# Row moments by VectorE transposes, and another order of the weight loads and stores, in a fused attention and MLP kernel

## The chip, the cores and the metric

The kernel runs on one core of a Trainium2 chip. The metric is the device time of one execution in microseconds (us), as a median of several runs. The engines of the core run side by side, each with an instruction stream of its own, and wait for each other by semaphores: TensorE (PE in the profile, with its weight loads as PEld), VectorE (DVE), ScalarE (ACT), GpSimd (POOL), and SyncE (SP), whose stream here holds nothing but the issue of DMA transfers.

## The reference

One batch of 2048 tokens of width 576 goes through two branches, which a gate mixes. All arrays are float32.

```python
x = A_x
g = _sigmoid((x * gate_w).sum(-1, keepdims=True))
a = _A_ref(x, A_wqkv, A_wo)            # linear attention, 32 heads of 18
b = _B_ref(x, B_w1, B_b1, B_w2, B_b2)  # layer norm, 576 -> 4608, gelu, 4608 -> 576
return g * a + (1 - g) * b
...
def _B_ref(x, w1, b1, w2, b2):
    y = _layernorm(x, axis=-1)
    h = _gelu(jnp.einsum("bsd,df->bsf", y, w1) + b1)
    return jnp.einsum("bsf,fd->bsd", h, w2) + b2
```

## The kernel before, in words

The tokens lie in 16 tiles of 128, which the kernel takes in eight pairs. Every large product is made by float32r matmuls on a value split in two: ACT copies a block to float32r (the high part), DVE subtracts that from the source (the low part), and three products of the parts are summed in PSUM. Both MLP products are also made by a seven-product scheme on 2x2 blocks, which trades matmuls for sums of blocks: A11, A12, A22 and the sums S1 to S4 of w1; B11, B12, B21, B22 and the sums T1 to T4 on the other side.

**The attention part** (the first 305 us) walks over the tiles. For a tile, PE projects keys and queries, ACT and DVE make the feature map, PE adds up the products of keys and x. In the same walk the mean and the scale of the layer norm are found. For pair q they stand in `mr[:, q]`, a tile of 128 partitions by 8 pairs by 2 kinds by 2 tiles: one number for a token, and the token is the partition. `share_moments` (line 383) stores them to a DRAM tensor `moments[q]` of 2 rows of 256 numbers, and `load_rows` (line 399) loads these rows back to all partitions, so that `normal_pair` can normalise x in its transposed form. Each pair's normalised and split blocks go to DRAM (`yd`) by `store_pair`; the first two blocks of w1 are also split here and stored (`w1d`, by `store_early`). All these transfers are issued by SP, in the order of the program.

**The MLP part** is 18 windows of 14 steps (line 1145), run after the attention part. A step holds seven matmuls of 512 columns of the first product (`product`) and twelve of 288 columns of the second (`unit`), which runs one window behind. Two blocks k of w1 belong to a window, one to its steps 0 to 6 and one to its steps 7 to 13. The first nine windows work on the first half of the tokens and the last nine on the second half. In the first half a block of w1 is loaded raw, summed, split, used, and stored in its split form to `w1d[k]`, from where the second half loads it back; so the second half has no sums and no splits of w1.

What runs beside the matmuls is written as jobs on the steps (lines 1049 to 1142), and on each engine the jobs stand in program order. For w1 in the first half, with x the first step of block k in its window:

- `sum_w1` of block k + 1 (DVE, four sums, 128x384) at x to x + 3, into a raw buffer `w1_raw` (`w_raw` in the profile). S1, S2 and S4 = A12 − S2 need what is called the early part here, the raw blocks that `load_w1(…, True)` loads; S3 = A11 − S3 needs the late part, one raw block that `load_w1(…, False)` loads into the place of S3.
- at x + 4 `split_w1(k + 1, True)` into `wa` (ACT, then DVE), and eight DMAs for the early part of block k + 2. At x + 5 the store of `wa` to `w1d`.
- at x + 6 the split of the other blocks into `wb`, and then four DMAs for the late part of block k + 2; at x + 7 the store of `wb`.

For w2 there is one buffer `w2r` of seven places. `load_w2(p + 1)` (line 919) loads the four blocks of the next window at step 5, into the places of operands that the window has used up. POOL makes the four sums T3, T1, T2, T4 (`sum_w2`, 128x576), and behind them in its stream the sums of h (`sum_h`, on the tile `u`). `prepare_hi`, `prepare_h_lo` and `prepare_w2_lo` split an operand pair of the second product two steps ahead of its use (ACT and DVE, tiles `h` and `w_ops`), at every second step.

Of the kernel before, what the change touches and what calls it, by code (L numbers as in the profile page):

```python
# [9 lines left out]
F32 = mybir.dt.float32  # L10
# [7 lines left out]
P = 128  # L18
# [53 lines left out]
A11, A12, S2, S1, S3, A22, S4 = range(7)  # L72
A21 = S3
FIRST_W, LAST_W = (A11, S1), (S3, S4)
B11, B21, T1, B22, T2, T3, T4 = range(7)
# [7 lines left out]
HALF_PAIRS = NCHUNK // 2  # L83
# [17 lines left out]
def half_cols(half):  # L101
    return slice(half * HALF, (half + 1) * HALF)
# [14 lines left out]
def tile_gated_mix(ctx: ExitStack, tc: tile.TileContext, x, xm, xe, wm, we, wvm, wve, wo, um, ue, w2, b1, b2, gw, out):  # L117
    nc = tc.nc
    pe, act, dve, pool = (InOrder(tc, e) for e in (nc.tensor, nc.scalar, nc.vector, nc.gpsimd))
    sp = InOrder(tc, nc.sync)  # L120

    keep = ctx.enter_context(tc.tile_pool(name="keep", bufs=1))
# [48 lines left out]
    acc += [acc_right[:, i * D:(i + 1) * D] for i in range(TPS)]  # L171
    b1s = keep.tile([P, NFT], F32, name="b1s")
    mr = keep.tile([P, NP, 2, 2], F32, name="mr")
    sumsq = keep.tile([P, NT], F32, name="sumsq")
    gsum = keep.tile([P, NT], F32, name="gsum")
    g = keep.tile([P, NT], F32, name="g")
# [4 lines left out]
    moments = [dram.tile([2, 2 * P], F32, name=f"moments{q}") for q in range(NP)]  # L181
# [10 lines left out]
    for part in (KEY, QUERY):  # L192
        for half in range(2):
            n = HALF + 2 * (part == KEY and half)
# [186 lines left out]
        dve.tensor_mul(r, r, vr)  # L381

    def share_moments(q):
        sp.dma_start(moments[q].rearrange("a (t n) -> n a t", n=P), mr[:, q])

    B12 = T1
# [206 lines left out]
    def prepare_scale(q, n):  # L595
        at(n, scale_in, q)
        at(n + 1, scale_out, q)
        at(n + 2, share_moments, q)
# [32 lines left out]
    for n, f in ((50, scale_in), (56, scale_out), (56, share_moments)):  # L631
        at(n, f, NP - 1)
# [277 lines left out]
    w2r = own_tile("w2r", [P, 7, 2, HALF], F32)  # L910
    w2_ops = own_tile("w2_ops", [P, 2, 2, 2, HALF], F32R)
    free_ups, ups_at, w2_at = list(range(7)), {}, {}
# [3 lines left out]
    H_SUMS = {S3: (H11, H21, OP.subtract), S2: (H22, H21, OP.subtract), S1: (H22, H11, OP.add), S4: (H12, H22, OP.subtract)}  # L916
    W2_SUMS = {T3: (B22, B12), T1: (B12, B11), T2: (B22, T1), T4: (B21, T2)}

    def load_w2(p):
        old = w2_at.get(p - 1)  # L920
        new = w2_at[p] = dict(zip((B11, B21, T1, B22, T3, T2, T4),
                                  [old[m] for m in (B11, B21, T4, T3, T2, T1, B22)] if old else range(7)))
        first = 2 * p % NCHUNK * CF * P
        rows_ = w2[first:first + 2 * CF * P].rearrange("(j f p) d -> f p j d", j=2, f=CF)
        for f, blocks_ in enumerate(((B11, B12), (B21, B22))):
            for half, m in enumerate(blocks_):
                sp.dma_start(w2r[:, new[m]], rows_[f][:, :, half_cols(half)])

    def sum_w2(p, m, by=pool):
        of = lambda n: w2r[:, w2_at[p][n]]  # L930
# [120 lines left out]
    def do(w, x, f, *args):  # L1051
        jobs.setdefault((w + x // 14, x % 14), ([], []))[1].append(lambda: f(*args))

    def do_first(w, x, f, *args):
        jobs.setdefault((w + x // 14, x % 14), ([], []))[0].append(lambda: f(*args))
# [11 lines left out]
    for p in range(WINDOWS - 1):  # L1067
        w = p + 1
        if p == 0:
            for x, m in ((11, T3), (12, T1), (13, T2), (14, T4)):  # L1070
                do(0, x, sum_w2, 0, m, dve)
        for m in range(7):
            x = 2 * m - 2 - 2 * (p == m == 0)
            do_first(w, x, prepare_hi, p, m)
            do(w, x, prepare_h_lo, p, m)
            do(w, x, prepare_w2_lo, p, m)
        for x, m in ((0, S3), (3, S2), (6, S1), (7, S4)):
            do(w, x, sum_h, p, m)
        for x, m in ((4, S3), (8, S2), (9, S1), (11, S4)):
            do(w, x, give_back, p, m)  # L1080
        do(w, 5, load_w2, p + 1)
        if p + 1 < WINDOWS - 1:
            for x, m in ((9, T3), (10, T1), (11, T2), (12, T4)):
                do(w, x, sum_w2, p + 1, m)

    for k in range(HALF_TIME):
        w, x = k // 2, 7 * (k % 2)
        if k >= EARLY:
            do(w, x - 1, split_w1, k, False)
            if k + 1 < HALF_TIME:  # L1090
                do(w, x - 1, load_w1, k + 1, False)
            do(w, x, store_w1, k, False)
        if EARLY <= k + 1 < HALF_TIME:
            for n, x1 in enumerate((0, 1, 2, 3)):
                do(w, x + x1, sum_w1, k + 1, n, dve)
            do(w, x + 4, split_w1, k + 1, True)
            if k + 2 < HALF_TIME:
                do(w, x + 4, load_w1, k + 2, True)
            do(w, x + 5, store_w1, k + 1, True)

    p = HALF_PAIRS - 1
    for x, n, t in ((5, 2, 1), (10, 6, 1), (11, 7, 6), (12, 6, 5), (12, 4, 7), (13, 7, 5), (14, 3, 6)):
# [9 lines left out]
    h_stage = h_ops.rearrange("p c k a n -> p (c k a n)")  # L1112
    h_stages = [stage_of(h_stage[:, n * 10 * P:(n + 1) * 10 * P]) for n in range(3)]
    do(0, 0, load_w2, 0)
    u_stage = ups[:, 4:7].rearrange("p a j n -> p (a j n)").bitcast(F32R)
    u_stages = [stage_of(u_stage[:, n * 10 * P:(n + 1) * 10 * P]) for n in range(2)]
# [6 lines left out]
    p, w = WINDOWS - 1, WINDOWS - 1  # L1123
# [21 lines left out]
    for w in range(WINDOWS):  # L1145
        for x in range(14):
            k, i = 2 * w + x // 7, x % 7
# [3 lines left out]
            n, opens = UP_ORDER[i], (1, 2, 5) if w else (1, 2, 5, 4)  # L1151
# [14 lines left out]
    p = WINDOWS - 1  # L1166
# [66 lines left out]
```

## Time and profile before

| | |
|---|---|
| median of 3 runs | 1159.26 us (1158.85 to 1162.0) |
| the profiled execution | 1160.28 us, its span 1158.6 us |
| busy share of the span | PE 95%, PEld 86%, DVE 75%, ACT 49%, POOL 35% |
| granted TensorE clock, mean | 0.994 |
| HBM traffic | 135.95 MB read, 69.09 MB written |
| sizes of single DMAs | `w2r` 288 KB, store of `wa` 1280 KB, of `wb` 960 KB, raw w1 128 KB and 64 KB |

The span runs from the first to the last instruction; the time of an execution holds 1.7 us more. In the rows of a timeline stand the start in us, the busy time in us, the engine, line and operation, the tiles as out<-in, and in brackets the idle time ahead of it with what ended it. Rows of equal instructions are merged and end in their count. All work is recorded by one helper, so nearly every row has line 113, and a row is told by its tiles. A row of stages gives the stretch, its length, the busy time of PE, PEld, DVE, ACT and POOL, then PE's granted clock, the DMA engines' busy share, and GB/s.

### The profile page before, as it was taken

To read this page: it belongs to the slowest core of one execution; us is meant where nothing else is said; L and a number is where in the kernel's file an instruction comes from. 1 tells how busy PE (TensorE), PEld (TensorE's weight loads), DVE (VectorE), ACT (ScalarE), POOL (GpSimd) and SP (SyncE) were. 2 spreads that over 40 slices of the span, in tenths; PEclk is the share of its full clock that TensorE was granted. 3 is DMA by queue.
4 is the path that set the end of the run, shared out by engine and by line. 5 is a ranking of instruction groups with operands and counts; after the bars stand their busy time and mean duration, and the time that the engine had idled before them with its cause. 6 is when DMAs were issued, how large, how long until landed. Compare 5 with 4: busy or idle time off the path is not lost.

```text
span 1158.6 us, 18002 instructions
## 1 busy us (share of the span) xinstructions
PE 1104.6 (95%) x6651; PEld 997.1 (86%) x6651; DVE 868.8 (75%) x1201; ACT 567.9 (49%) x917; POOL 401.0 (35%) x276
## 2 busy tenths in 40 slices
PE   8988999899899999999998999999999999999998
PEld 8978898799777888888787888988999999999998
DVE  4676888798486979888798888688666666666587
ACT  6655675244464545445454554445444444444450
POOL 1101112783223333344233434425324424334310
PEclk9999999999999999999999999999999999999999
DMA  6489988886854364543546458856444344344342
GB/s 179 130 213 260 197 193 183 190 315 229 279 207 162 131 212 148 194 161 121 179 140 222 159 178 317 322 154 235 129 117 145 110 136 143 103 144 143 105 155 82
DMA packets 131133, 206.22 MB, mean 178 GB/s; under 512 B 13935, under 2 KB 86895, under 8 KB 127078
## 3 DMA queue, kind: packets, MB, share of 16 engines
q1 hardware_dynamic: 130482, 204.49, 56.9%
q8 instruction: 52, 0.85, 0.3%
q10 hardware_dynamic: 564, 0.59, 0.2%
q14 instruction: 35, 0.29, 0.1%
HBM read 135.95 MB, written 69.09 MB: 177 GB/s over the span
## 4 chain that ended last, share of the span: by engine, by line
PE 57%; DVE 18%; DMA 12%; issue 5%; SPq 4%; ACT 3%; POOL 0%; ACTq 0%; DVEq 0%; POOLq 0%
PE ps L113 57%; SPq L113 4%; DMA w_raw<-in_ue 4%; DVE wa L113 3%; DVE h L113 3%; DVE accs L113 3%; DVE w_ops L113 3%; DMA yd<-ys 1%; DMA w_raw<-in_um 1%; DVE den L113 1%; DMA w2r<-in_w 1%; ACT wa L113 1%; DMA xn<-in_x 1%; DMA wv<-in_wve 1%; DMA late_acc<-acc_right 1%
## 5 line engine op out<-in xcount | busy, mean ns | idle before, releaser
L113 PEld LDWEIGHTS ps<-w_ops,h 128*128 128x128 f32 x2856 | 429.0, 188 | 71.1 <-DVE w_ops L113 28.0
L113 PE MATMUL ps<-w_ops,h 128*128 128x288 f32 x2856 | 462.2, 297 | 21.2 <-DVE w_ops L113 19.2
L113 POOL TENSOR_TENSOR u<-u 128x512 f32<-128x512 f32 x136 | 212.8, 1592 | 273.0 <-DVE h L113 152.1
L113 PE MATMUL ps<-y,wa 128*128 128x512 f32 x1008 | 280.9, 395 | 5.7 <-DVE wa L113 2.8
L113 DVE TENSOR_TENSOR accs<-ps,accs 128x576 f32<-128x576 f32 x210 | 158.5, 755 | 98.7 <-PE ps L113 91.9
L113 ACT ACTIVATE u<-u,b1s 128x512 f32<-128x512 f32 x110 | 79.7, 725 | 269.3 <-DVE u L113 269.3
L113 PE MATMUL ps<-y,wb 128*128 128x512 f32 x756 | 203.3, 394 | 0.2
L113 PEld LDWEIGHTS ps<-y,wa 128*128 128x128 f32 x1008 | 173.7, 188 | 30.1 <-DVE wa L113 6.7
L113 POOL TENSOR_TENSOR w2r<-w2r 128x576 f32<-128x576 f32 x64 | 96.5, 1508 | 228.1 <-DMA w2r<-in_w 105.9
L113 PE MATMUL ps<-y 128*128 128x288 f32 (+1 forms) x1088 | 154.4, 300 | 14.8 <-DVE k L113 10.6
L113 PEld LDWEIGHTS ps<-y 128*128 128x128 f32 x1088 | 150.0, 191 | 19.1 <-DVE k L113 12.3
L113 DVE TENSOR_TENSOR h<-u,h 128x1024 fp32r<-128x1024 f32 x119 | 157.0, 1319 | 2.7 <-ACT h L113 2.6
L113 PEld LDWEIGHTS ps<-y,wb 128*128 128x128 f32 x756 | 132.8, 188 | 19.2 <-DVE u L113 0.7
L113 ACT ACTIVATE h<-u 128x1024 fp32r<-128x1024 f32 x119 | 125.1, 1051 | 39.3 <-PE ps L113 39.2
L113 ACT ACTIVATE u<-ps 128x512 f32<-128x512 f32 x110 | 64.8, 591 | 88.8 <-PE ps L113 88.7
L113 DVE TENSOR_TENSOR w_ops<-w2r,w_ops 128x576 fp32r<-128x576 f32 x119 | 108.0, 907 | 0.0
L113 DVE TENSOR_TENSOR u<-ps,u 128x512 f32<-128x512 f32 x110 | 75.4, 686 | 37.3 <-PE ps L113 24.3
L113 ACT ACTIVATE w_ops<-w2r 128x576 fp32r<-128x576 f32 x119 | 79.7, 670 | 0.0
L113 DVE TENSOR_TENSOR w_raw<-w_raw 128x384 f32<-128x384 f32 x64 | 53.8, 841 | 32.0 <-DMA w_raw<-in_ue 18.0
L113 PE MATMUL ps<-wp,qt 128*128 128x288 f32 x448 | 64.8, 302 | 2.7 <-DVE qt L113 2.7
L113 PEld LDWEIGHTS ps<-wp,qt 128*128 128x128 f32 x448 | 61.4, 192 | 2.9 <-DVE qt L113 2.9
L113 POOL TENSOR_TENSOR pks<-pks,k 128x576 f32<-128x576 f32 x15 | 21.8, 1455 | 103.4 <-DVE k L113 103.3
(136 smaller groups left out, 886.3 us busy)
## 6 DMA issues: line engine op xcount, KB each, us to landing
wa<-w1d SPq DMA_DIRECT2D x80, 320.0 KB
w2r<-in_w SPq DMA_DIRECT2D x72, 288.0 KB
w1d<-wa SPq DMA_DIRECT2D x16, 1280.0 KB
wb<-w1d SPq DMA_DIRECT2D x60, 320.0 KB
y<-yd SPq DMA_DIRECT2D x14, 1280.0 KB
w1d<-wb SPq DMA_DIRECT2D x16, 960.0 KB
w_raw<-in_um SPq DMA_DIRECT2D x96, 128.0 KB
yd<-ys SPq DMA_DIRECT2D x15, 640.0 KB
```

Source lines behind the costliest of these rows:

```text
L113: return lambda *args, **kwargs: self.tc.keep_in_program_order(op(*args, **kwargs))
```

## The change

Three things are changed; no matmul, no ACT instruction and no POOL instruction is added, removed or put elsewhere in its engine's stream.

**Moments.** `mr` is cleared at the start. For a pair, DVE turns four 32x32 blocks of `mr` (all eight pairs' columns of 32 partitions each) into a tile `mrt` of 32 partitions by 128, and SP stores four rows of 128 numbers instead of 128 times 4 single numbers.

**w2.** The four blocks of the next window are loaded one by one, in the first half at steps 1, 1, 3 and 4 instead of all at 5. The steps of `sum_w2` are renumbered one or two lower, which leaves POOL's stream as it was.

**Late part of w1.** The store of `wa` is issued behind the loads of the late part instead of ahead of them, and S4 is summed ahead of S3.

```diff
     def share_moments(q):
-        sp.dma_start(moments[q].rearrange("a (t n) -> n a t", n=P), mr[:, q])
+        for n in range(0, P, 32):
+            dve.transpose(mrt[:, n:n + 32], mr[n:n + 32].rearrange("p q k a -> p (q k a)"))
+        sp.dma_start(moments[q].rearrange("k (a n) -> (k a) n", a=2), mrt[4 * q:4 * q + 4])
...
-        do(w, 5, load_w2, p + 1)
+        if p + 1 < HALF_PAIRS:
+            for x, m in ((1, B11), (1, B21), (3, B12), (4, B22)):
+                do(w, x, load_w2, p + 1, (m,))
+        else:
+            do(w, 5, load_w2, p + 1)
...
             do(w, x - 1, split_w1, k, False)
             if k + 1 < HALF_TIME:
                 do(w, x - 1, load_w1, k + 1, False)
+            do(w, x - 1, store_w1, k, True)
             do(w, x, store_w1, k, False)
         if EARLY <= k + 1 < HALF_TIME:
-            for n, x1 in enumerate((0, 1, 2, 3)):
+            for x1, n in zip((0, 1, 2, 3), (0, 1, 3, 2)):
                 do(w, x + x1, sum_w1, k + 1, n, dve)
             do(w, x + 4, split_w1, k + 1, True)
             if k + 2 < HALF_TIME:
                 do(w, x + 4, load_w1, k + 2, True)
-            do(w, x + 5, store_w1, k + 1, True)
```

The first place is SP's stream in window 1, behind the eight early loads that are issued at step 4. Before, the four blocks of w2, the store of `wa` and the late part (four rows of `w_raw`) stand there in this order:

```order
L113 DMA w_raw<-in_ue 128x1x128
L113 DMA w2r<-in_w 128x2x288 x4
L113 DMA w1d_109<-wa 128x2560
L113 DMA w_raw<-in_um 128x2x128
L113 DMA w_raw<-in_ue 128x1x128
L113 DMA w_raw<-in_um 128x2x128
L113 DMA w_raw<-in_ue 128x1x128
L113 DMA w1d_109<-wb 128x1920
```

In SP's stream now, the blocks of w2 stand right behind the stores of the block before, ahead of the early loads (two of the eight are shown):

```order
L113 DMA w1d_110<-wa 128x2560
L113 DMA w1d_110<-wb 128x1920
L113 DMA w2r<-in_w 128x2x288 x4
L113 DMA w_raw<-in_um 128x2x128
L113 DMA w_raw<-in_ue 128x1x128
```

and behind the last early loads SP's stream has the late part, then both stores:

```order
L113 DMA w_raw<-in_ue 128x1x128
L113 DMA w_raw<-in_um 128x2x128
L113 DMA w_raw<-in_ue 128x1x128
L113 DMA w_raw<-in_um 128x2x128
L113 DMA w_raw<-in_ue 128x1x128
L113 DMA w1d_111<-wa 128x2560
L113 DMA w1d_111<-wb 128x1920
```

So the late part has moved in front of 4 x 288 KB of w2 and of 1280 KB of `wa`. It still waits for the split of `wb`, whose raw source it overwrites. (The name `w1d_111` is the same tensor as `w1d_109` before, by another number.)

The second place is DVE's stream in the attention part, behind the scale of the second pair. Before, DVE goes from the split of w1 (`ys`) to the query features (`accs<-ps,e`):

```order
L113 TENSOR_TENSOR xs<-xn,xs 128x512
L113 TENSOR_TENSOR xs<-xn,xs 128x64
L113 TENSOR_TENSOR ys_550<-acc_right,ys_550 128x2x256
L113 TENSOR_TENSOR ys_550<-acc_right,ys_550 64x2x128
L113 SCALAR_TENSOR_TENSOR accs<-ps,e 128x288 x2
```

and DVE now has four transposes between them:

```order
L113 TENSOR_TENSOR ys_552<-acc_right,ys_552 128x2x256
L113 TENSOR_TENSOR ys_552<-acc_right,ys_552 64x2x128
L113 STREAM_TRANSPOSE mrt<-mr 32x32 x4
L113 SCALAR_TENSOR_TENSOR accs<-ps,e 128x288 x2
L113 TENSOR_TENSOR ys_553<-acc_right,ys_553 128x2x256
```

Such four stand at eight places, one for each pair; apart from them and the clearing of `mr` at the start, DVE's stream differs only in the swap of two sums of w1, which read alike. SP's store of the moments has kept its place, and waits for the transposes.

More of the change, by code (lines that the diff above doesn't have):

```diff
@@ L173, in tile_gated_mix @@
     mr = keep.tile([P, NP, 2, 2], F32, name="mr")
+    dve.memset(mr, 0.0)
+    mrt = keep.tile([32, P], F32, name="mrt")
     sumsq = keep.tile([P, NT], F32, name="sumsq")
@@ L917, in tile_gated_mix, with load_w2 @@
     W2_SUMS = {T3: (B22, B12), T1: (B12, B11), T2: (B22, T1), T4: (B21, T2)}
[L919 to L922, printed above, removed]
+    def load_w2(p, blocks_=(B11, B12, B21, B22)):
+        if p not in w2_at:
+            old = w2_at.get(p - 1)
+            w2_at[p] = dict(zip((B11, B21, T1, B22, T3, T2, T4),
+                                [old[m] for m in (B11, B21, T4, T3, T2, T1, B22)] if old else range(7)))
         first = 2 * p % NCHUNK * CF * P
         rows_ = w2[first:first + 2 * CF * P].rearrange("(j f p) d -> f p j d", j=2, f=CF)
-        for f, blocks_ in enumerate(((B11, B12), (B21, B22))):
-            for half, m in enumerate(blocks_):
-                sp.dma_start(w2r[:, new[m]], rows_[f][:, :, half_cols(half)])
+        for m in blocks_:
+            f, half = divmod((B11, B12, B21, B22).index(m), 2)
+            sp.dma_start(w2r[:, w2_at[p][m]], rows_[f][:, :, half_cols(half)])
     def sum_w2(p, m, by=pool):
@@ L1076, in tile_gated_mix @@
             do(w, x, prepare_w2_lo, p, m)
-        for x, m in ((0, S3), (3, S2), (6, S1), (7, S4)):
+        for x, m in ((0, S3), (3, S2), (6, S1), (7, S4)) if p < HALF_PAIRS else ((0, S3), (3, S2), (6, S1), (7, S4)):
             do(w, x, sum_h, p, m)
@@ L1080, in tile_gated_mix @@
             do(w, x, give_back, p, m)
-        do(w, 5, load_w2, p + 1)
+        if p + 1 < HALF_PAIRS:
[3 more added lines that the diff above has]
+            do(w, 5, load_w2, p + 1)
         if p + 1 < WINDOWS - 1:
-            for x, m in ((9, T3), (10, T1), (11, T2), (12, T4)):
+            for x, m in ((8, T3), (9, T1), (10, T2), (12, T4)) if p + 1 < HALF_PAIRS else ((9, T3), (10, T1), (11, T2), (12, T4)):
                 do(w, x, sum_w2, p + 1, m)
```

## The prediction

> **What bounds the kernel now.** I read the stages first, then the waits, then the rows around the longest waits. This table cuts the span at the places where the work changes:
>
> ```profile
> 52.00:75.00 23.00, 18.10 (x113) 17.01 (x112) 15.39 (x36) 12.93 (x30) 3.27 (x3) 0.93 0.69 195
> 75.00:210.00 135.00, 126.81 (x836) 119.06 (x836) 106.84 (x227) 80.10 (x183) 23.78 (x20) 1.00 0.89 203
> 210.00:230.00 20.00, 14.83 (x81) 12.42 (x80) 16.66 (x23) 4.96 (x11) 15.51 (x11) 0.97 0.84 217
> 230.00:305.00 75.00, 73.34 (x537) 71.96 (x536) 59.36 (x103) 35.68 (x76) 41.09 (x27) 0.98 0.75 257
> 305.00:701.27 396.27, 370.78 (x2067) 319.49 (x2066) 328.43 (x391) 200.28 (x267) 143.94 (x92) 0.99 0.50 174
> 701.27:1158.60 457.33, 452.24 (x2717) 411.20 (x2717) 314.81 (x366) 201.85 (x281) 164.68 (x108) 1.00 0.50 160
> ```
>
> PE is nearly full everywhere, so only its idle time and its stretched windows can be won: 25.5 us idle from 305 to 701 us (396.27 − 370.78), where w1 is summed and split, 5.2 us from 210 to 230, 8.2 from 75 to 210, 4.9 from 52 to 75. Two windows of the first half and one (the last row) without sums of w1:
>
> ```profile
> 551.47:601.23 49.76, 46.78 (x266) 40.57 (x267) 41.72 (x51) 24.40 (x32) 18.57 (x12) 1.00 0.47 165
> 601.23:651.52 50.29, 46.73 (x266) 40.60 (x267) 43.60 (x51) 24.36 (x32) 19.09 (x12) 1.00 0.46 162
> ...
> 701.27:746.10 44.83, 44.77 (x265) 40.23 (x265) 32.82 (x39) 21.14 (x29) 18.59 (x12) 1.00 0.93 364
> ```
>
> The same 265 or so matmuls take 44.8 us there and 49.8 to 50.3 here: PE loses 5 us a window to something else. That is DVE, whose busy time is 42 to 44 us. Its longest waits from 305 to 701 us:
>
> ```profile
> DVE w_raw L113 <- DMA w_raw<-in_ue: 18.0, 7, 3.6
> DVE wa L113 <- ACT wa L113: 12.0, 8, 1.5
> DVE wb L113 <- ACT wb L113: 11.3, 9, 2.4
> DVE w_raw L113 <- issue: 9.2, 6, 2.4
> DVE w_raw L113 <- DMA w_raw<-in_um: 4.7, 1, 4.7
> ```
>
> The sums of w1 wait 31.9 us (18.0 + 9.2 + 4.7) for raw w1, in seven windows: 4.6 us each. Of `w_raw <- issue` the named cause is unsure; I take it for the early part, which is the only thing that sum needs. In one window:
>
> ```profile
> 558.74 0.56 DVE L113 TENSOR_TENSOR w_raw<-w_raw 128x384 f32<-128x384 f32 x1 [1.22 <-issue]
> ...
> 567.09 0.81 DVE L113 TENSOR_TENSOR w_raw<-w_raw 128x384 f32<-128x384 f32 x1 [3.59 <-DMA w_raw<-in_ue]
> ...
> 569.62 0.75 DVE L113 TENSOR_TENSOR w_ops<-w2r,w_ops 128x576 fp32r<-128x576 f32 x1
> ```
>
> PE then waits for that `w_ops`, and once more a little later, since DVE is still late:
>
> ```profile
> 570.42 0.80 PE L113 MATMUL ps<-w_ops,h 128*128 128x288 f32 x4 [1.27 <-DVE w_ops L113]
> ...
> 578.20 0.79 PE L113 MATMUL ps<-w_ops,h 128*128 128x288 f32 x4 [1.11 <-DVE w_ops L113]
> ```
>
> **Late part of w1, and w2.** Why the late part is late shows in SP's rows:
>
> ```profile
> 555.45 2.46 SPq L113 DMA_DIRECT2D w2r<-in_w  x4
> 557.95 0.47 SPq L113 DMA_DIRECT2D w1d<-wa  x1
> 558.51 0.38 SPq L113 DMA_DIRECT2D w_raw<-in_um  x1
> ...
> 561.45 1.57 SPq L113 DMA_DIRECT2D w_raw<-in_ue  x1
> ```
>
> Four pieces of w2 (1.15 MB) and the store of `wa` (1.28 MB) are issued ahead of it; 2.4 MB at the rate of a full queue (415 GB/s in a row further down) are about 6 us. In the change both are gone from there: the late part is issued when `wb` is split, about 557 us (step 6, right ahead of the sum at 558.74), and only early loads of 0.77 MB lie before it. I estimate it landed by 561 to 562, and its sum stands one step (3.5 us) later, behind S4. So the 3.59 us wait goes. The 1.22 us wait for the early part stays in principle: those eight loads are issued as before, since the last piece of w2, which now stands ahead of them, waits for an operand split at step 4 that DVE makes before the split of `wa` that the early loads wait for anyway. The other three pieces go out at steps 1 and 3, where SP has nothing else to issue. The store of `wa` waits, in SP's order, for the split of `wb` and for four more issues: some 1.3 us.
>
> What is late next is POOL against DVE. With w2 there early, POOL starts T3 and T1 at step 6 and T2 at step 8, when the operands whose places they take are split, and not when the loads land. Before, one window had these sums inside DVE's wait, another had them beside its work:
>
> ```profile
> 563.03 4.45 POOL L113 TENSOR_TENSOR w2r<-w2r 128x576 f32<-128x576 f32 x3 [13.41 <-DMA w2r<-in_w]
> ...
> 612.80 5.00 POOL L113 TENSOR_TENSOR w2r<-w2r 128x576 f32<-128x576 f32 x3 [13.43 <-DVE h L113]
> ```
>
> ```profile
> 613.22 1.78 DVE L113 TENSOR_TENSOR w_raw<-w_raw 128x384 f32<-128x384 f32 x1
> ...
> 616.74 1.48 DVE L113 TENSOR_TENSOR w_raw<-w_raw 128x384 f32<-128x384 f32 x1 [1.07 <-DMA w_raw<-in_ue]
> ```
>
> In the first, all three sums (563.03 to 567.48) lay in the 3.59 us in which DVE waited, and cost it little. In the second, the DVE sums took 1.78 and 1.48 us instead of 0.56: a POOL sum beside a DVE operation from SBUF costs DVE 0.9 to 1.2 us. That is why the window with the shorter wait is no shorter (50.29 us against 49.76), and DVE's busy time is 1.9 us higher there. In the changed kernel there is no long wait to hide in. The unknown is how many of the three sums meet such an operation: none, and all 4.6 us are won; three, and 0.9 us is left (4.6 − 3 x 1.22). I take two, as in the second window: 4.6 − 2.4 = 2.2 us a window. PE's two waits above, 2.4 us, agree with that as what DVE's lateness costs it; beyond them PE keeps what it loses at steps 3 to 5 to POOL's sums of h, which the change leaves alone. Seven windows: **15.5 us**, with bounds of 6.3 (7 x 0.9) and 31.9.
>
> A rule speaks here against the change. The Trainium skill (page "SBUF — State Buffer", section "SBUF: two separate sides") says that DVE and GpSimd share a port pair as an exclusive lock, and that the loser is blocked for the whole instruction. By that rule each of the three sums could cost DVE its full 1.48 us (4.45 / 3), 4.4 us in all, and a window would win 0.2 us. The rows above, 0.9 to 1.2 us for a collision, show part of that.
>
> **Moments.** The store of the first pair's moments, 512 single numbers, goes out at 52.35 us, and then the queue is slow:
>
> ```profile
> 52.35 0.60 SPq L113 DMA_DIRECT2D moments<-mr  x1
> ...
> 56.92 3.60 SPq L113 DMA_DIRECT2D w1d<-ys  x2
> ```
>
> ```profile
> 60.00:62.00 2.00, 2.00 (x13) 1.87 (x12) 1.25 (x4) 1.85 (x4) 0.00 (x0) 1.00 0.43 35
> 62.00:64.00 2.00, 2.00 (x17) 2.00 (x16) 1.90 (x4) 0.16 (x1) 0.00 (x0) 1.00 0.59 98
> 64.00:66.00 2.00, 2.00 (x16) 1.96 (x15) 0.80 (x4) 0.00 (x0) 0.81 (x1) 1.00 1.03 415
> 112.00:114.00 2.00, 0.00 (x0) 0.00 (x0) 1.14 (x3) 1.94 (x6) 0.00 (x0) 1.00 1.41 47
> ```
>
> At 60 to 64 us the DMA engines are half busy and move 35 and 98 GB/s, though 1.28 MB wait in the queue; then it flows at 415. The last row is the same dip behind the third pair's store. Who waits for the stores of `ys` is ACT, which writes that buffer next, then DVE, then PE:
>
> ```profile
> 68.30 0.84 ACT L113 ACTIVATE ys<-acc_right 128x768 fp32r<-128x768 f32 x1 [6.14 <-issue]
> ```
>
> ```profile
> 69.17 1.15 DVE L113 TENSOR_TENSOR ys<-acc_right,ys 128x512 fp32r<-128x512 f32 x2 [4.36 <-ACT ys L113]
> ```
>
> ```profile
> 72.47 0.85 PE L113 MATMUL ps<-y 128*128 128x288 f32 x2 [4.90 <-DVE k L113]
> ```
>
> With four rows of 512 bytes the dip should go, and with it DVE's 4.36 us; PE's 4.90 shrinks by about **4.0** (bounds 0, if ACT waits for something else, and 4.9). Behind the third pair's store PE waits 1.21 us at 127.14:
>
> ```profile
> 127.14 1.07 PE L113 MATMUL ps<-y 128*128 128x288 f32 x6 [1.21 <-DVE k L113]
> ```
>
> I count **0.7** for it (0 to 1.2). The other dips fall where PE is full, except the seventh pair's, ahead of 210 us: the loads behind it feed POOL's normalising, which then runs beside DVE at 210 to 230, where PE idles 5.2 us. If POOL starts sooner, part of that goes: **1.5** (0 to 4, and −1 if POOL then meets other work).
>
> The price is 32 transposes on DVE. Nothing in the trace is a transpose; the nearest are the smallest operations on the same tile:
>
> ```profile
> L113 DVE TENSOR_TENSOR mr<-mr,mt x8: 161/162/841, 51.9 to 225.7; 128x2 f32<-128x2 f32 x8
> ```
>
> At 0.16 us four take 0.65 us a pair, 5.2 in all; at the 0.84 of the slowest, 3.4 us a pair and 27 in all. I take 0.16: that 0.84 was beside POOL. From 75 to 210 us DVE is busy 79% and PE 94%, so most of it lies under matmuls; I charge **1.0** (two pairs, where PE waits for DVE), with bounds 0 and 5.2. The Trainium skill ("VectorE: DVE Perf Modes", section "The three transpose paths") gives 311 ns for all blocks of a 128x128 bf16 tile; an estimate from that would be at most 0.3 us for a pair's four, and the charge would be 0.5.
>
> **Sum.** 15.5 + 4.0 + 0.7 + 1.5 − 1.0 = 20.7 us, against the profiled execution's 1160.28: 1139.6. That execution lies 1.0 above the median of the runs shown (1159.26), so the forecast is 1138.6.
>
> **Rivals.**
>
> *POOL takes the place of the wait.* All three w2 sums block DVE; a window wins 0.9 us or less, 6 in all, and with the attention part's 5.2 the time is 1148. For it: the 50.29 us window. Against: with the early w2 the sums spread over steps 6 to 8, beside PSUM operations too. Chance 0.2. The lock rule of the "SBUF — State Buffer" page of the Trainium skill would take this to its end, 0.2 x 7 + 5.2 and so 1153; 0.05 of the 0.2 stands for it.
>
> *DVE is on time everywhere.* The sums fall beside PSUM operations and ACT waits; a window wins 3.5 us, 24.5 in all, and the attention part 8: 1127. Chance 0.12.
>
> *The late part is no earlier.* If its issue is held by something other than what stands ahead of it, the 3.59 us wait stays and only the attention part gains: 1154. Against: SP's four issues of it at 558.51 to 563.02 stretch as in a full queue. Chance 0.03.
>
> *The store of `wa` comes too late (slower).* It now goes behind the late part, with the store of `wb` at its heels. ACT rewrites `wa` at step 4 of the next block; in this window:
>
> ```profile
> 572.10 1.47 ACT L113 ACTIVATE wa<-w_raw 128x1536 fp32r<-128x1536 f32 x1
> ```
>
> Issued at about 559 instead of 557.95, and wanted some 2.4 us sooner, the store has about 10 us for 1.28 MB, of which it needs some 3 at 415 GB/s. From there on, each us stops ACT, and DVE and PE behind it, in each of 15 blocks: 1.4 us too late eat the 20.7, and at 2 us too late the time is 1139 + 30 = 1169. Against: the queue carries 165 GB/s on average. Chance 0.03.
>
> The rest, 0.62, is the forecast's own case.
>
> **Chances.** A measurement of this kernel can tell about 0.3% (3.5 us). Faster by more: 0.93; within: 0.03; slower: 0.04. The range takes the bounds of windows from 8 to 25 us with the attention part from 2 to 8: 1127 to 1149.
>
> **What would show it.** Right: DVE's waits for `w_raw` fall from 31.9 us to under 10; windows of about 47.5 us; POOL's `w2r` sums start at step 6 and no longer wait for a DMA; no dip in GB/s at 60 us and PE's 4.90 us under 1.5. Wrong: the sums of w1 still wait for `w_raw`; DVE's busy time in a window over 46 us; ACT waiting for `w1d<-wa`; transposes of over 0.5 us.

## The result, and the profile after

The changed kernel, called after here, takes 1130.13 us (median of 4 runs, 1129.0 to 1130.98), the kernel before 1159.63 us on the same chip (4 runs, 1158.85 to 1162.0). The ratio is 0.9742, with a 95% interval of 0.9723 to 0.976: 29.5 us less, where 20.7 were forecast. The profiled execution took 1130.96 us, its span is 1129.2 us.

The stages of after, cut where the same work begins and ends. The first window with a steady rhythm begins at 344.17 us (352.64 before) and the last row's at 671.94 us (701.27 before):

```profile
52.00:75.00 23.00, 21.85 (x144) 20.25 (x142) 20.40 (x50) 16.31 (x36) 3.69 (x3) 1.00 0.74 239
75.00:207.00 132.00, 124.40 (x814) 115.98 (x815) 107.77 (x243) 77.89 (x177) 29.05 (x23) 1.00 0.61 204
207.00:232.00 25.00, 23.38 (x155) 20.98 (x154) 21.85 (x42) 9.51 (x23) 18.88 (x13) 1.00 0.88 336
...
344.17:671.94 327.77, 322.60 (x1863) 283.70 (x1863) 301.10 (x345) 173.70 (x230) 136.74 (x84) 1.00 0.51 175
671.94:1129.20 457.26, 452.25 (x2717) 411.28 (x2717) 314.74 (x366) 201.82 (x281) 164.60 (x108) 1.00 0.50 160
```

The same cuts of before:

```profile
207.00:232.00 25.00, 19.83 (x110) 17.07 (x109) 19.42 (x34) 6.51 (x16) 17.51 (x12) 0.94 0.84 203
...
352.64:701.27 348.63, 328.06 (x1863) 285.55 (x1863) 292.34 (x345) 173.85 (x230) 131.30 (x84) 1.00 0.49 168
```

The seven windows took 348.63 us and take 327.77: 49.80 us each became 46.82, and 20.9 us are won. Everything ahead of them ends 8.5 us sooner (352.64 − 344.17): 7.2 us are won by the first matmul of the MLP part (298.22, then 291.03 us), the rest in the first windows. Behind them nothing moved: 457.33 us before, 457.26 now. Note that DVE's busy time in the seven windows rose, from 292.34 to 301.10 us, while PE's idle time fell from 20.6 (348.63 − 328.06) to 5.2 us.

DVE's waits from 297 to 690 us; the 31.9 us for raw w1 are gone, and what is left is the same two waits for ACT, and waits for PE:

```profile
DVE wa L113 <- ACT wa L113: 12.0, 8, 1.5
DVE wb L113 <- ACT wb L113: 11.2, 9, 2.4
DVE accs L113 <- PE ps L113: 6.7, 16, 2.1
...
DVE w_raw L113 <- DMA w_raw<-in_ue: 0.3, 1, 0.3
```

One window of after, POOL's sums T3 and T1 of w2 and DVE's rows from there on (steps 6 to 10; T2 runs from 542.45 to 544.07 us):

```profile
535.03 3.79 POOL L113 TENSOR_TENSOR w2r<-w2r 128x576 f32<-128x576 f32 x2 [5.73 <-DMA w_raw<-in_um]
```

```profile
534.87 2.65 DVE L113 TENSOR_TENSOR wb<-w_raw,wb 128x768 fp32r<-128x768 f32 x2
537.55 0.76 DVE L113 TENSOR_TENSOR accs<-ps,accs 128x576 f32<-128x576 f32 x1
538.29 0.95 DVE L113 TENSOR_TENSOR w_raw<-w_raw 128x384 f32<-128x384 f32 x1
...
543.37 1.12 DVE L113 TENSOR_TENSOR w_raw<-w_raw 128x384 f32<-128x384 f32 x1
544.68 0.76 DVE L113 TENSOR_TENSOR accs<-ps,accs 128x576 f32<-128x576 f32 x1 [0.19 <-PE ps L113]
```

T3 and T1 start at step 6, as forecast. The split of `wb` beside them takes 2.65 us instead of 1.54, two sums of w1 take 0.95 and 1.12 us instead of 0.56: 2.1 us, nearly the 2.4 charged. But in front of the sum at 538.29 there is no wait any more for the early part (1.22 us before): the slow split fills it. And at 544.68 DVE waits for PE: it is on time.

In the attention part, the flow of data behind the first pair's store, and the row where PE waited 4.90 us:

```profile
60.00:62.00 2.00, 2.00 (x14) 1.88 (x13) 1.80 (x4) 1.58 (x4) 0.00 (x0) 1.00 0.66 269
62.00:64.00 2.00, 2.00 (x16) 1.98 (x15) 1.85 (x4) 1.16 (x3) 0.00 (x0) 1.00 0.96 326
```

```profile
68.42 3.99 PE L113 MATMUL ps<-y 128*128 128x288 f32 x28 [0.58 <-DVE k L113]
```

35 and 98 GB/s became 269 and 326, and the matmuls that began at 72.47 begin at 68.42 us.

### The profile page after: what moved, and what is told of

Its sections match the earlier page's. It is cut to its first block, busy times and chain, and to the rows that moved or that the text cites. A ratio compares the mean times of both kernels' runs of the same rounds, so it can differ in the third digit from the quotient of the medians.

```text
span 1129.2 us, 18023 instructions
## 1 busy us (share of the span) xinstructions
PE 1099.8 (97%) x6651; PEld 995.1 (88%) x6651; DVE 879.9 (78%) x1234; ACT 568.2 (50%) x917; POOL 406.1 (36%) x276
## 4 chain that ended last, share of the span: by engine, by line
PE 70%; DVE 16%; DMA 5%; issue 4%; ACT 2%; SPq 2%; POOL 0%; DVEq 0%; ACTq 0%; POOLq 0%
PE ps L113 70%; DVE accs L113 3%; DVE h L113 3%; DVE wa L113 2%; DVE w_ops L113 2%; SPq L113 2%; DVE ys L113 1%; DMA w_raw<-in_ue 1%; DVE wb L113 1%; DMA xn<-in_x 1%; DMA t<-in_xe 1%; DVE u L113 1%; DMA wa<-w1d 1%; DVE y L113 1%; DMA yd<-u 1%
## 5 line engine op out<-in xcount | busy, mean ns | idle before, releaser
L113 POOL TENSOR_TENSOR w2r<-w2r 128x576 f32<-128x576 f32 x64 | 101.9, 1592 | 202.2 <-DVE w_ops L113 67.3
L113 DVE TENSOR_TENSOR accs<-accs 128x384 f32<-128x384 f32 (+3 forms) x59 | 52.9, 903 | 4.0 <-issue 1.6
```

Source lines behind the costliest of these rows:

```text
L113: return lambda *args, **kwargs: self.tc.keep_in_program_order(op(*args, **kwargs))
```

## The experiments

Twelve kernels, in three groups. The medians of the kernel before beside each group were 1160.82, 1160.13 and 1160.16 us; each ratio is against its own, and what a half of the change gains is taken from its ratio.

**One half of the change each.** First the kernel before with the moments turned and stored in rows, and nothing else:

```
+    dve.memset(mr, 0.0)
+    mrt = keep.tile([32, P], F32, name="mrt")
...
-        sp.dma_start(moments[q].rearrange("a (t n) -> n a t", n=P), mr[:, q])
+        for n in range(0, P, 32):
+            dve.transpose(mrt[:, n:n + 32], mr[n:n + 32].rearrange("p q k a -> p (q k a)"))
+        sp.dma_start(moments[q].rearrange("k (a n) -> (k a) n", a=2), mrt[4 * q:4 * q + 4])
```

> Only the moments are turned and stored as four rows; w2 and w1 are handled as in the kernel before. Theory (the two halves of the change add, and the attention part gained the 8.5 us by which the first window starts earlier): 1159.6 - 8.5 = 1151, with windows still 49.8 us apart and the 4.90 us wait of PE near 72 us under 1. Rival (the forecast's sizes): 4.0 + 0.7 + 1.5 - 1.0 = 5.2 us, 1154.4. Second rival (part of the 8.5 us came from w2 or w1 moving): under 4 us, above 1155.

Measured: 1151.9 us, ratio 0.9927 (0.9915 to 0.9939), 8.5 us less. Then the other half: after, with the moments as in before.

> Only w2 in early single pieces, the stores behind the late part and the late sum one step later; moments stored number by number as before. Theory: seven windows at 46.9 instead of 49.8 us, 20.9 us, so 1138.7; the attention part stays as before, first window at 305 us. Rival (the forecast's size): 15.5 us, 1144. If the parts helped each other, this gain and that of the moments alone would not add up to 29.5 us.

Measured: 1138.6 us, ratio 0.9817 (0.9801 to 0.9833), 21.2 us less; its seven windows take 327.85 us. 0.9927 x 0.9817 is 0.9745, and the whole change gave 0.9742: the halves add, and both are larger than forecast (5.2 and 15.5).

**Inside the windows: w2, or the late part?** The kernel before with w2 alone in early single pieces, its sums at steps 8, 9 and 10 (one lower each than before), the stores and the order of the sums of w1 as they were:

```
-        do(w, 5, load_w2, p + 1)
+        if p + 1 < HALF_PAIRS:
+            for x, m in ((1, B11), (1, B21), (3, B12), (4, B22)):
+                do(w, x, load_w2, p + 1, (m,))
+        else:
+            do(w, 5, load_w2, p + 1)
...
```

> The kernel before with w2 alone changed (four single pieces at steps 1, 1, 3, 4, its sums at steps 8, 9, 10). Theory (the queue ahead of the late part sets the wait): 1.15 of the 2.43 MB are gone from in front of it, some 2.8 us of the 3.6, so the wait of the sums of w1 falls from 31.9 to about 12 us and a window wins about 2: 1145. Rival (the store of wa alone holds the late part back): the wait stays over 25 us and the gain is under 4 us: 1156 or more. Second rival (POOL's sums, now free to run beside DVE, eat what the wait gives back): the wait falls, DVE's busy time in a window rises by as much, 1157 to 1160.

And the kernel before with only the late part ahead of the stores and S4's sum ahead of S3's, w2 at step 5:

```
             do(w, x - 1, split_w1, k, False)
             if k + 1 < HALF_TIME:
                 do(w, x - 1, load_w1, k + 1, False)
+            do(w, x - 1, store_w1, k, True)
             do(w, x, store_w1, k, False)
...
-            for n, x1 in enumerate((0, 1, 2, 3)):
+            for x1, n in zip((0, 1, 2, 3), (0, 1, 3, 2)):
...
-            do(w, x + 5, store_w1, k + 1, True)
```

> The kernel before with the late part of w1 issued in front of both stores and its sum one step later; w2 loaded at step 5 as before, in front of it. Theory (queue): 1.28 of the 2.43 MB are gone from in front, some 3 us, and the sum comes 3.5 us later, so the 3.59 us wait goes whole, while POOL's sums still wait for w2 and fall where they fell: a window wins 2 to 2.9 us, 1139 to 1146. Rival (w2 in front is what holds it): the sum still waits 2 us or more and the gain is under 8 us: above 1151.

Measured: 1139.57 us (0.9822, 0.9809 to 0.9835) and 1149.95 us (0.9915, 0.9896 to 0.9934). The seven windows of the first, and of the second:

```profile
349.90:677.74 327.84, 322.70 (x1863) 283.64 (x1863) 299.59 (x345) 173.75 (x230) 136.81 (x84) 1.00 0.52 175
```

```profile
351.76:689.77 338.01, 324.97 (x1862) 284.50 (x1863) 302.36 (x345) 174.10 (x230) 136.69 (x84) 1.00 0.49 173
```

The early w2 alone gives all that the windows won (327.84 against 327.85 us with everything). With w2 gone from in front of it, the late part lands in time although the 1.28 MB of `wa` still go first; the moved stores and the swapped sums then add nothing. By themselves they give half, 48.29 us a window. My theory, which counted MB in the queue, missed both times: 1145 expected for the first, 1139 to 1146 for the second. Nor was the second's rival right, by which w2 in front holds the late part: DVE's wait for raw w1 had fallen to 10 us there too, and its rows show one wait in each window, in front of the first sum (step 7), which needs the early part; no sum waits for the late part any more. So either move alone brings the late part in time. (Whether in the second it was the place of the store or the later sum was not tried.) The second kernel falls short by another loss. DVE's rows at step 10, and POOL's:

```profile
558.41 1.54 DVE L113 TENSOR_TENSOR h<-u,h 128x1024 fp32r<-128x1024 f32 x1
559.87 1.99 DVE L113 TENSOR_TENSOR w_ops<-w2r,w_ops 128x576 fp32r<-128x576 f32 x1
```

```profile
555.72 5.52 POOL L113 TENSOR_TENSOR w2r<-w2r 128x576 f32<-128x576 f32 x3 [13.07 <-DMA w2r<-in_w]
```

The three sums wait for w2 and then run in one go, beside the splits of `h` and `w_ops` for which PE waits (1.22 and 0.75 us elsewhere; the second expectation below puts them at step 8). So is it w2's transfer that costs, or where the late w2 puts POOL? Both kernels, with the early w2 (after) and with the late one, were run without T3, T1 and T2:

```
-                do(w, x, sum_w2, p + 1, m)
+                if p + 1 >= HALF_PAIRS or m == T4:
+                    do(w, x, sum_w2, p + 1, m)
```

> The changed kernel without the three sums T3, T1 and T2 of w2 on POOL in the windows of the first half (left out, so the products with them are of other numbers). Theory (where those sums now run, their cost to DVE fills a wait for the early part of w1 and slack behind it, and PE's remaining loss comes from the sums of h at steps 3 to 5): windows stay at 46.8 us within 0.3, 1128 to 1131; DVE waits about 1 us for the early part in each window. Rival (the forecast's: two collisions of 1.2 us each reach PE): a window falls by 1 to 2.4 us to the floor of 44.8, 1113 to 1123.

> The kernel with the late part in front of the stores and w2 at step 5, without the sums T3, T1 and T2 of w2 in the first half (left out). It tells why w2 at step 5 costs 1.46 us a window more (48.29 against 46.83 us). Theory (the sums of w2, held back by the loads, fall on the splits of h and of w2 at step 8, 1.54 and 1.99 us instead of 1.22 and 0.75, on top of a wait of 1.2 us that they no longer fill): without them windows are 46.8 us and the time 1140. Rival (the transfers of w2 in the queue are what costs): windows stay at 48 us or more, 1148 to 1150.

Measured: 1128.77 us (0.9725, 0.9712 to 0.9739) with the early w2, and 1137.96 us (0.9811, 0.9796 to 0.9826) with the late one. Their seven windows, in that order:

```profile
342.61:668.04 325.43, 321.75 (x1863) 284.12 (x1863) 286.09 (x345) 174.74 (x230) 100.27 (x63) 1.00 0.51 176
```

```profile
350.53:678.78 328.25, 322.24 (x1862) 284.10 (x1863) 286.02 (x345) 173.95 (x230) 100.16 (x63) 1.00 0.51 178
```

Both theories hold, though 46.49 us lies at the lower edge of the first. Where the early w2 puts them, the sums cost DVE 15.0 us (301.10 − 286.09), 2.1 us a window, but the windows only 2.3 us in all (327.77 − 325.43), 0.33 each; without the sums DVE waits 8.5 us more for the early part, 1.2 us a window. At step 10 they cost DVE 2.3 us a window and PE 1.4 (338.01 − 328.25, over 7). The transfers of w2 at step 5 cost little: without POOL's sums a window is 46.89 us with them there, 46.49 without.

**What holds the windows now.** POOL's sums of h run beside DVE's steps 2 to 4, and two splits of step 4 take 1.85 and 3.02 us where they take 0.74 and 1.93 without POOL beside them (rows further down):

```profile
519.23 10.07 POOL L113 TENSOR_TENSOR u<-u 128x512 f32<-128x512 f32 x6 [8.41 <-DVE h L113]
```

```profile
526.31 1.85 DVE L113 TENSOR_TENSOR w_ops<-w2r,w_ops 128x576 fp32r<-128x576 f32 x1
528.08 3.02 DVE L113 TENSOR_TENSOR wa<-w_raw,wa 128x1024 fp32r<-128x1024 f32 x2
```

After without S1 and S4 of h on POOL, four of these six instructions:

```
-        for x, m in ((0, S3), (3, S2), (6, S1), (7, S4)) if p < HALF_PAIRS else ((0, S3), (3, S2), (6, S1), (7, S4)):
+        for x, m in ((0, S3), (3, S2)) if p + 1 < HALF_PAIRS else ((0, S3), (3, S2), (6, S1), (7, S4)):
```

> The changed kernel without the sums S1 and S4 of h (four of POOL's six instructions at steps 1 to 4) in the first half (left out). Theory (these are what keeps the windows 2 us above the 44.83 us floor: the w_raw, h, w_ops and wa operations beside them took 0.4 to 1.1 us longer): windows of 45.0 to 45.7, 1130.1 - 7 x 1.5 = about 1120. Rival (the windows are held by DVE's load as such, 43 of 47 us): 46.5 or more, 1128 to 1130.

Measured: 1115.95 us (0.9618, 0.9605 to 0.9631). Its seven windows, with PE busy without a gap:

```profile
336.42:651.34 314.92, 314.92 (x1863) 284.54 (x1862) 280.75 (x344) 176.49 (x231) 89.21 (x56) 1.00 0.53 182
```

44.99 us a window: nearly all of the rest of the loss was these two sums of h. In the windows of after no engine shows a wait that POOL ended, so it is what they cost DVE, whose busy time fell by 20.35 us (301.10 − 280.75), and not their own lateness. The kernel needs them, but the same lesson says where to put one: S4 behind T3 and T1.

```
-        for x, m in ((0, S3), (3, S2), (6, S1), (7, S4)) if p < HALF_PAIRS else ((0, S3), (3, S2), (6, S1), (7, S4)):
+        for x, m in ((0, S3), (3, S2), (6, S1), (8, S4)) if p + 1 < HALF_PAIRS else ((0, S3), (3, S2), (6, S1), (7, S4)):
...
-            for x, m in ((8, T3), (9, T1), (10, T2), (12, T4)) if p + 1 < HALF_PAIRS else ...
+            for x, m in ((7, T3), (7, T1), (10, T2), (12, T4)) if p + 1 < HALF_PAIRS else ...
```

> The changed kernel with the sum S4 of h put behind T3 and T1 on POOL (steps 7, 7, 8), in the first half: all work is done, in another order. Theory (two of the collisions at steps 4 and 5, with w_ops and wa, 1.1 us each, leave the place where PE waits for them, and fall on steps 7 and 8, where DVE has slack): windows of 45.8 to 46.5 us, 1123 to 1128. Rival (steps 7 and 8 have no slack, since the sums of w1 stand there): windows of 47 us or more, 1131 to 1136.

Measured: 1120.74 us (0.9658, 0.9644 to 0.9671), with all work done, and so faster than both kernels: 9.4 us under the changed one. Its seven windows, POOL's shorter row beside DVE's steps 2 to 4, the two splits of step 4, and the one wait that PE has left in a window:

```profile
334.56:654.96 320.40, 316.99 (x1864) 284.94 (x1863) 292.49 (x345) 176.08 (x232) 128.92 (x85) 1.00 0.52 179
```

```profile
512.23 6.09 POOL L113 TENSOR_TENSOR u<-u 128x512 f32<-128x512 f32 x4 [8.41 <-DVE h L113]
525.85 3.79 POOL L113 TENSOR_TENSOR w2r<-w2r 128x576 f32<-128x576 f32 x2 [7.54 <-DMA w_raw<-in_um]
529.60 2.87 POOL L113 TENSOR_TENSOR u<-u 128x512 f32<-128x512 f32 x2
```

```profile
519.32 0.74 DVE L113 TENSOR_TENSOR w_ops<-w2r,w_ops 128x576 fp32r<-128x576 f32 x1
519.98 1.93 DVE L113 TENSOR_TENSOR wa<-w_raw,wa 128x1024 fp32r<-128x1024 f32 x2
```

```profile
534.42 0.79 PE L113 MATMUL ps<-w_ops,h 128*128 128x288 f32 x4 [0.66 <-DVE w_ops L113]
```

45.77 us a window. The theory had half of it: the collisions did not only move to a place with slack, they became fewer. DVE's busy time in the windows fell by 8.6 us (301.10 − 292.49); at its new place S4 meets a sum of w1 (1.15 us at 530.15) and otherwise operations that read PSUM. The last wait of PE seemed to come from a 1.01 us wait of DVE for the early part, a step ahead of it, so the sums of w1 were put a step later:

```
-            for x1, n in zip((0, 1, 2, 3), (0, 1, 3, 2)):
+            for x1, n in zip((1, 2, 3, 3), (0, 1, 3, 2)):
```

> The kernel with S4 of h behind T3 and T1, and the sums of w1 at steps 1, 2, 3, 3 instead of 0, 1, 3, 2 of a block: all work is done. Theory (PE's last wait in a window, 0.66 us for w_ops at step 8, comes from DVE's 1.01 us wait for the early part in front of it, which goes when the sum stands a step later): 7 x 0.66 = 4.6 us less, windows of 45.2 to 45.5 us, 1116. Rival (the sums, now closer to the split that needs them, make wa late at step 4): PE waits for wa by 0.5 us or more a window, 1121 to 1125.

Measured: 1132.28 us (0.9761, 0.9743 to 0.9778), 11.5 us worse, 47.25 us a window. DVE's wait went as expected, but PE did not wait less. DVE's rows at step 8:

```profile
538.82 1.67 DVE L113 TENSOR_TENSOR h<-u,h 128x1024 fp32r<-128x1024 f32 x1
540.41 1.85 DVE L113 TENSOR_TENSOR w_ops<-w2r,w_ops 128x576 fp32r<-128x576 f32 x1
```

With the sum of w1 gone from step 7, these splits of `h` and `w_ops` come sooner and fall beside POOL's S4 (538.11 to 541.64 us); PE then waits 0.52 us here, no less than before. The larger loss stands two steps ahead of the window's end:

```profile
547.12 2.26 DVE L113 TENSOR_TENSOR w_raw<-w_raw 128x384 f32<-128x384 f32 x2
552.14 1.95 DVE L113 TENSOR_TENSOR wa<-w_raw,wa 128x1024 fp32r<-128x1024 f32 x2 [1.50 <-ACT wa L113]
```

```profile
556.73 0.79 PE L113 MATMUL ps<-w_ops,h 128*128 128x288 f32 x4 [1.21 <-DVE w_ops L113]
```

Two sums of w1 now stand right ahead of the split of `wa`, beside POOL's T4, where the kernel without this step has one of 0.55 us. ACT starts `wa` 8.3 us behind PE's wait at step 8 (550.64 − 542.31) instead of 6.6 (541.04 − 534.42), and on DVE the `w_ops` for which PE waits stands behind `wa`. So the rival had the direction, and for this wait the reason: `wa` comes late, only that PE meets it through `w_ops`. The theory had been read from one window: DVE waited for the early part in two of the seven (1.8 us in all), PE for `w_ops` six times (3.4 us).

**Inside the moments: the store, or the turning?** After with the rows stored, but without the transposes (the tile is filled with a constant instead); and the kernel before with the transposes added and the old store kept. The first edit:

```
+    dve.memset(mrt, 0.5)
...
         for n in range(0, P, 32):
-            dve.transpose(mrt[:, n:n + 32], mr[n:n + 32].rearrange("p q k a -> p (q k a)"))
+            pass
```

> The changed kernel with the moments stored as four rows but without the 32 transposes (left out, the rows hold a constant, so the normalising is of other numbers). Price of the transposes. Theory (they lie under matmuls but for two pairs): 0.3 to 1 us, so 1129 to 1130. Rival (0.84 us of DVE a pair reaches PE in every pair): 6.7 us, 1123.5.

> The kernel before with the transposes added and their result not used: the moments are still stored number by number. Theory (the store alone brings the gain, the transposes cost 0 to 1 us): 1159.6 to 1161. Rival (0.84 us a pair reaches PE): 1166. A time under 1158 would mean that the turning itself helps.

Measured: 1126.62 us (0.9714, 0.9698 to 0.973), 3.5 us under the changed kernel, and 1162.3 us (1.0018, 1.0007 to 1.0028), 2.1 us above the kernel before. So the turning costs 2 to 3.5 us and not the 1.0 charged, and the rows alone are worth 12.0 us (1138.6 − 1126.62). The transposes in after, with the fastest, the middle and the slowest in ns; then a wait of PE in after, and last the same place without the transposes:

```profile
L113 DVE STREAM_TRANSPOSE mrt<-mr x32: 192/199/203, 54.3 to 218.2; 32x32 f32<-32x32 f32 x32
```

```profile
176.52 3.70 PE L113 MATMUL ps<-y 128*128 128x288 f32 x26 [1.39 <-DVE k L113]
```

```profile
173.84 3.97 PE L113 MATMUL ps<-y 128*128 128x288 f32 x28 [0.16 <-DVE k L113]
```

Last, the store of single numbers doubled in the kernel before:

```
         sp.dma_start(moments[q].rearrange("a (t n) -> n a t", n=P), mr[:, q])
+        sp.dma_start(again[q].rearrange("a (t n) -> n a t", n=P), mr[:, q])
```

> The kernel before with each pair's moments stored number by number twice, the second time to a place that nobody reads. Theory (512 single numbers hold up what is queued behind them; the places where PE waits are the first and third pair's and the stretch behind 210 us): as much again as the four rows took away, 8 us or more, 1167 to 1172. Rival (what the four rows won was the way of the moments from their store to their load, not the queue): 1159 to 1162.

Measured: 1161.26 us (1.0019, 1.0005 to 1.0034): 2.2 us more by the ratio, where I expected 8 or more. My theory that each such store holds up the queue by its own numbers falls. The flow in this kernel:

```profile
60.00:62.00 2.00, 2.00 (x14) 1.89 (x13) 1.28 (x3) 1.59 (x4) 0.00 (x0) 1.00 0.61 31
62.00:64.00 2.00, 2.00 (x16) 1.98 (x15) 1.87 (x4) 0.41 (x1) 0.00 (x0) 1.00 0.37 49
64.00:66.00 2.00, 2.00 (x17) 2.00 (x16) 1.06 (x4) 0.00 (x0) 0.81 (x1) 1.00 0.79 272
```

```profile
73.12 5.68 PE L113 MATMUL ps<-y 128*128 128x288 f32 x28 [5.30 <-DVE k L113]
```

PE begins only 0.65 us later (73.12 against 72.47). The dip looks alike, but SP's row shows that it is not the same: the first store of `ys`, issued at 56.92 us before, goes out here at 63.82, and SP's wait of 6.7 us in front of it is put down to an earlier DMA. So for most of this dip the 1.28 MB that wait in the kernel before were not in the queue at all. ACT's row names the stores of `ys`, which the prediction had only taken for the cause, as what ACT waits for:

```profile
63.82 1.76 SPq L113 DMA_DIRECT2D w1d<-ys  x2
```

```profile
68.96 0.84 ACT L113 ACTIVATE ys<-acc_right 128x768 fp32r<-128x768 f32 x1 [6.55 <-DMA w1d<-ys]
```

That the store of single numbers makes the dip of the kernel before is shown by its going with the rows; why it lasts as long as it does, and why twice the numbers cost so little more, stays open. For the first pair the rival is out, since nobody waits for a load of moments at 72 us. Behind the seventh pair's store SP's rows speak for the queue too. Two loads of x, which need no moments and are issued ahead of the load of moments, take SP 5.28 us in before and 1.12 in after:

```profile
201.36 5.28 SPq L113 DMA_DIRECT2D accs<-in_xe  x2
```

```profile
194.86 1.12 SPq L113 DMA_DIRECT2D accs<-in_xe  x2
```

How much of the later gains comes from there, and how much from the way of the moments, was not measured apart.

## Why the prediction was right, and where its sizes were not

Direction, mechanism and range held: the waits for raw w1 went (31.9 us, then 0.3), POOL's sums of w2 start at step 6, the dip at 60 us is gone, nothing waits for the store of `wa`. The gain was 8.8 us larger than forecast; 5.4 of them sit in the windows and about 3.3 ahead of them.

- **Windows: 15.5 forecast (seven times 2.2 is 15.4), 20.9 measured (2.98 us each).** The step that failed is "I take two, as in the second window: 4.6 − 2.4 = 2.2 us". The collisions came, on three operations, and cost DVE 2.1 us a window (shown by leaving the sums out). But the subtraction took DVE's loss for PE's. One collision falls on the split of `wb`, in front of the 1.22 us wait for the early part that the forecast itself had left in place, and fills it; PE loses 0.33 us. What then stops a window short of the 44.83 us floor is what the text had named, POOL's sums of h: without two of them a window is 44.99 us.
- **The late part.** The text put four pieces of w2 and the store of `wa` ahead of it, about 6 us of transfers, and took both away. Either would have done: with the store still ahead, DVE waits 2.4 us in six windows together, and with w2 still ahead (and S3's sum a step later), no sum waits for the late part. What w2's early load wins beyond that is not the queue but POOL's place: its sums leave step 10, where they cost PE 1.4 us a window. The forecast treated the two moves as one and so could not see that, with w2 loaded early, moving the store adds nothing.
- **First pair's store: 4.0 forecast, 4.05 measured** (72.47 to 68.42).
- **Third pair, 210 to 230 us, transposes: 0.7 + 1.5 − 1.0 = 1.2 forecast, 4.4 measured** (8.5 less the first pair's 4.05). Two errors of opposite sign. Transposes took 0.199 us each, not 0.16, and 2 to 3.5 us of their 6.4 reached PE: it waits for DVE at more places than the two pairs counted (0.71 us at 75.14 and 1.03 at 220.70 are gone without the transposes, 2.42 at 109.55 and 1.39 at 176.52 are 1.76 and 0.16). Against that, the rows without their turning gave 12.0 us instead of 6.2. POOL's normalising starts at 201.36 instead of 213.57 us, as the text guessed; at 228.78 us PE's group begins 8.1 us sooner (220.70):

```profile
228.78 4.45 PE L113 MATMUL ps<-wp,qt 128*128 128x288 f32 x20 [2.66 <-DVE qt L113]
```

```profile
220.70 2.92 PE L113 MATMUL ps<-wp,qt 128*128 128x288 f32 x20 [1.03 <-DVE qt L113]
```

Of the rivals, "DVE is on time everywhere" came nearest in number (3.5 us a window, 1127), but by luck: its reason was that POOL's sums fall beside PSUM operations, and they fell on `wb` and `w_raw`, in time that DVE had to spare. "POOL takes the place of the wait" describes the kernel with the late part moved and w2 not: there POOL's sums do cost PE 1.4 us a window. For the rule of an exclusive lock (the Trainium skill, page "SBUF — State Buffer", section "SBUF: two separate sides") the runs give a number: POOL's T3, T1 and T2 take 5.4 us in a window of after (3.79 + 1.62 for T2 at 542.45), and DVE loses 2.1 us, so it isn't blocked for the whole of each. That does not refute the rule, since the sums and DVE's operations overlap only in part, and the runs do not show which had the ports first. That page counts DVE operations with two inputs in SBUF among those that compete for the lock; the trace agrees (last section). The estimate from "The three transpose paths" (page "VectorE: DVE Perf Modes" of the Trainium skill), at most 0.3 us a pair, was too low: a pair's four took 0.8 us.

## What to carry to other kernels

A collision of two engines costs what it costs the engine that the end waits for, and only there: ask what stands behind the slowed instruction before its next wait. Moving one of POOL's sums away from the splits for which PE waits won 9.4 us more here, with all work done. Moving sums of w1 a step later to take away a wait seen in one window lost 11.5, since other splits then stood beside POOL and `wa` came late. When several things stand ahead of a late transfer, move them one at a time: here either move brought it in time, and one of them gave the whole gain of the windows.

## What the runs showed of the hardware that was not expected

DVE's operations that read PSUM kept their time beside POOL (`accs` 0.76 us at 537.55, with T1 running), while those with both sources in SBUF took 0.3 to 1.2 us longer (`w_raw`, `h`, `w_ops` in the rows above); none lost as much as a whole POOL instruction (1.6 to 1.9 us).

Some gaps of PE were followed by a lower clock. In the kernel before, PE waits for `qt` from 226.1 to 228.8 us, and the granted clock in the stretches behind it is 0.72 and 0.50; in after, 1.00 (second fence):

```profile
226.00:228.00 2.00, 0.11 (x1) 0.00 (x0) 1.93 (x5) 0.00 (x0) 1.24 (x2) 1.00 0.13 1
228.00:230.00 2.00, 1.22 (x5) 1.23 (x6) 1.94 (x3) 0.00 (x0) 1.92 (x3) 0.72 2.55 82
230.00:232.00 2.00, 2.00 (x11) 2.00 (x10) 1.74 (x4) 1.54 (x5) 2.00 (x2) 0.50 0.90 36
```

```profile
230.00:232.00 2.00, 2.00 (x17) 2.00 (x16) 1.97 (x2) 0.31 (x1) 2.00 (x2) 1.00 1.01 425
```

Not every gap was: behind PE's 3.21 us ahead of 114.35 us, in the same run, the clock is 1.00. Why the one and not the other stays open.
